# Reordering scores, x transposes, exponentials and masks in the opening of a fused attention and feed-forward kernel

## The chip, the cores and the metric

The kernel runs on one core of a Trainium2 chip. The metric is the device time of one execution in microseconds; of several runs the median is given.

## The reference

Sliding-window attention over 8 batches, 8 heads, 576 positions and a head width of 64 (each position sees those at most 32 away), followed by a two-layer feed-forward block with the quick GELU:

```python
scores = scale * np.matmul(q, k.transpose(0, 1, 3, 2))
mask = np.abs(pos[:, None] - pos[None, :]) <= window
scores = np.where(mask, scores, -1000000000.0)
scores = scores - np.max(scores, axis=-1, keepdims=True)
attn = np.exp(scores)
attn = attn / (np.sum(attn, axis=-1, keepdims=True) + 1e-09)
x = (attn @ v).transpose(0, 2, 1, 3).reshape(4608, 512)
h = x @ w_in
out = (h * (1.0 / (1.0 + np.exp(-1.702 * h)))) @ w_out
```

w_in is 512x2048, w_out 2048x512.

## The kernel before, in words

The 4608 rows are cut into 36 units of 128 rows. Four units make a tile of 512 rows, and the feed-forward block works on tiles. One unit goes through these steps:

- `scores(u, tag)`: 24 small matmuls into two PSUM banks (heads of even and of odd number), then two exponentials on ScalarE (L263), one for each bank, into the SBUF tile p.
- `band(u)`: one multiplication by the 0/1 mask on VectorE (L271), over both halves of p. It needs both exponentials.
- `odd_v(u, eng)`: two copies (L216 and L217) that put together the tile vo from the second half of value tile ve of unit u and the first half of that of unit u+1. In the opening most of them are on VectorE, later they are on GpSimd.
- `values(u, tag)`: 16 small matmuls (pv) into two banks, with a column of ones that yields the sums of the softmax.
- `norm(u)`: reciprocal and multiplication on VectorE (L300, L301), which give x. In the two-bank form "t" that is one pair of instructions, in the forms "AC" and "BE" two pairs.
- `x_T2(u, tag, eng)`: eight transposes on TensorE for units u and u+1 (L329) into one bank, and one copy (L67) to xT.

PSUM has eight banks, and the kernel names them: "t" is two banks, then A, C, B, E, LA and LB. A bank that is asked for again can be written once all instructions that read its last content are done.

The layers use a scheme of seven products of half-sized blocks. In layer 1 (`l1_group`) the sums of the x blocks come from `x_sums` on VectorE, and the order on TensorE is products 1, 7, 6, 2, 5, 4, 3; between 7 and 6 ScalarE copies bank A to B and C to an SBUF tile (L67). Layer 2 (`layer2`) is a list of single matmuls, 8 for each product (o<-w,g; o<-b,g; o<-b,gs and so on), that is drawn from with `do(more, n)` to fill TensorE while other engines work. After the 8 matmuls of product 7 come two copies of seeds, by the engine in `seed2` (L67, o<-o and s7o<-o); product 6 accumulates onto the first one. After product 2 a copy (L521) by the engine in `l2eng` takes a quarter of the result to SBUF.

The order is written out by hand. Each engine runs its instructions strictly in the order of the program (`manual_schedule`), and semaphores are set from the data. So the order of the calls in `opening` (units 0 to 7), `first_layer1` and `run` (units 8 to 15 up to `back(2)`) is the order on every engine.

Loads are issued on the GpSimd queue (`load_v`, `load_w2`, `load_kq`), and each one names one of eight semaphores in turn, so that a load also waits for the one eight places ahead of it. Transposes of q and k by DMA and the stores are on SyncE's queue.

Of the kernel before, what the change touches and what calls it, by code (L numbers as in the profile page):

```python
# [19 lines left out]
AF = mybir.ActivationFunctionType  # L20
# [6 lines left out]
class _Kernel:  # L27
# [214 lines left out]

    def scores(self, u, tag):
        kT, q = self.kT[u], self.qT[u]
        nxt = self.k_first if u == self.NU - 1 else self.kT[u + 1][:, :, 0:64]
        if tag == "t":
            sc = self.bank(tag, name="sc")
            sc = [sc[:, 0], sc[:, 1]]  # L250
        else:
            sc = [self.bank(x, name="sc") for x in tag]
        for hp in range(4):
            c = 128 * hp
            for eo in range(2):
                r = slice(64 * eo, 64 * eo + 64)
                lo, hi = sc[eo][0:64], sc[eo][64:128]
                self.mm(lo[:, c:c + 64], kT[r, hp, 0:64], q[r, hp, 0:64], start=(hp == 0))
                self.mm(hi[:, c:c + 128], kT[r, hp, 64:128], q[r, hp, :], start=(hp == 0))
                self.mm(lo[:, c + 64:c + 128], nxt[r, hp, :], q[r, hp, 64:128], start=False)  # L260
        p = self.p[u] = self.sb("p", [128, 2, 8, SQ], BF16, 4)
        for eo in range(2):
            self.nc.scalar.activation(p[:, eo].rearrange("k h s -> k (h s)"), sc[eo], AF.Exp, scale=self.scale)  # L263

    def band(self, u, eng=None):
        p = self.p[u]
# [302 lines left out]
    def opening(self):  # L569

        nc, dve, act, pool = self.nc, self.nc.vector, self.nc.scalar, self.nc.gpsimd
        self.setup()
        dve.memset(self.idle, 0.0)
        dve.memset(self.spark, 0.0)
        for t in self.ve:
            dve.memset(t[:, :, self.D:], 1.0)
        self.load_first("k", 0)
        self.load_first("q", 0)
        make_identity(nc, self.ident)
        act.activation(self.spark, self.spark, AF.Exp)  # L580
        for u in (0, 1, 2):
            self.load_v(u)
        self.load_w1(0)
        self.setup_mask()
        self.load_first("k", 1)
        self.load_first("q", 1)
        self.cut_mask()
        self.load_w1(1)
        self.load_v(3)
        self.load_v(4)  # L590
        self.load_w1(2)
        self.load_four("k")
        self.load_four("q")
        self.load_w1(3)
        self.odd_v(3, pool)
        dve.tensor_copy(self.identh, self.ident)
        self.keep_busy(60, "E", 96)
        self.T_first("k", 0, "AC", (dve, act))
        self.keep_busy(6, "E")
        self.T_first("q", 0, ("LA", "LB"), (dve, act))  # L600
        self.keep_busy(4, "E")
        for u in (5, 6):
            self.load_v(u)
        self.load_w2(0)
        self.load_v(7)
        self.load_v_part(1024, 64)
        self.load_w2(1)
        self.load_v_part(1088, 64)
        for c in (2, 3):
            self.load_w2(c)  # L610
        self.load_kq("k", 8)
        self.scores(0, "t")
        self.scores(1, "AC")
        self.odd_v(0, dve)
        self.odd_v(1, dve)
        self.keep_busy(10, "E")
        self.band(0)
        self.band(1)
        self.values(0, "t")
        self.values(1, "AC")  # L620
        self.norm(0)
        self.norm(1)
        self.keep_busy(6, "E")
        self.x_T(0, "LA", act)
        self.keep_busy(4, "E")
        self.x_T(1, "LB", act)
        self.T_first("k", 1, "AC", (dve, dve))
        h, n, gelus = [], [0], []

        def l1(half, *ds):  # L630
            for d in ds:
                self.layer1_plain(0, d, half, h[n[0] % len(h)])
                n[0] += 1

        self.layer1_plain(0, 0, 0, "B", gelus)
        self.T_first("q", 1, ("LA", "LB"), (dve, act))
        self.layer1_plain(0, 1, 0, "E", gelus)
        h[:] = ["B", "E", "LB", "LA", "B", "E", "LB", "LA"]
        self.scores(2, "t")
        self.scores(3, "AC")  # L640
        self.layer1_plain(0, 2, 0, "LA", gelus)
        self.layer1_plain(0, 3, 0, "LB", gelus)
        self.do(gelus)
        self.band(2)
        self.odd_v(2, dve)
        self.band(3)
        self.keep_busy(4, "t")
        self.values(2, "t")
        self.norm(2)
        self.keep_busy(4, "A")  # L650
        self.values(3, "AC")
        self.norm(3)
        l1(0, 4)
        self.x_T2(2, "A", dve)
        l1(0, 5)
        dve.tensor_copy(self.k_first, self.kT[0][:, :, 0:64])
        dve.tensor_copy(self.v_first, self.ve[0][0:64])
        for i in (3, 1, 2):
            self.w1_sums((i,), 0)
        for u in (8, 9, 10, 11):  # L660
            self.fetch(u)
        l1(1, 0, 1)
        halo = self.kT[4]
        self.T_four("k", "AC", (dve, dve))
        dve.tensor_copy(self.kT[4][:, :, 0:64], halo)
        self.w1_sums((4,), 0)
        l1(1, 2, 3)
        self.T_four("q", "AC", (dve, act))
        l1(1, 4, 5)
        self.odd_v(4, dve)  # L670
        self.scores(4, "t")
        self.scores(5, "AC")
        self.odd_v(5, dve)
        for i in (3, 1):
            self.w1_sums((i,), 1)
        for d, tag in ((6, "B"), (7, "E")):
            self.layer1_plain(0, d, 0, tag, gelus)
        self.do(self.l2, 3)
        self.scores(6, "t")
        self.do(self.l2, 3)  # L680
        self.scores(7, "AC")
        self.do(gelus)
        self.do(self.l2, 2)
        self.band(4)
        self.odd_v(6, dve)
        self.odd_v(7, dve)
        self.band(5)
        self.values(4, "t")
        self.norm(4)
        self.band(6)  # L690
        self.values(5, "AC")
        self.norm(5)
        self.band(7)
        self.do(self.l2, 4)
        self.values(6, "t")
        self.norm(6)
        self.do(self.l2, 4)
        self.values(7, "AC")
        self.norm(7)
        h[:] = "BE"  # L700
        n[0] = 0
        l1(1, 6, 7)
        self.x_T2(4, "A", act)
        self.do(self.l2, 4)
        self.x_T2(6, "t", dve)
        self.do(self.l2, 4)
# [10 lines left out]
    @staticmethod  # L717
    def do(fs, n=99):
        for _ in range(min(n, len(fs))):
            fs.pop(0)()  # L720
# [77 lines left out]
    def run(self):  # L798
        pool, act = self.nc.gpsimd, self.nc.scalar
        self.l2 = self.layer2_plain(0, 0) + self.layer2_plain(0, 1)  # L800
        self.opening()
        self.do(self.x_sums(1))
        late = self.first_layer1()
        more = self.layer2([(i, j) for i in range(1, self.NT) for j in range(2)][:-1], (self.NT - 1, 1))
        do = self.do
        self.l2eng = dve = self.nc.vector
        self.seed2 = act
        self.scores(8, "t")
        self.scores(9, "AC")
        self.turn(14)  # L810
        self.turn(15)
        do(late, 2)
        do(self.l2)
        self.l2 = more
        self.scores(10, "BE")
        do(more, 12)
        self.band(8)
        self.band(9)
        do(late)
        do(more, 4)  # L820
        self.values(8, "t")
        self.values(9, "AC")
        self.odd_v(12, pool)
        self.odd_v(13, pool)
        self.fetch(16)
        self.fetch(17)
        self.norm(8)
        self.norm(9)
        do(more, 8)
        self.band(10)  # L830
        self.scores(11, "BE")
        do(more, 8)
        self.x_T2(8, "t", act)
        self.values(10, "AC")
        self.norm(10)
        do(more, 8)
        self.scores(12, "t")
        self.scores(13, "BE")
        self.band(11)
        self.values(11, "AC")  # L840
        self.norm(11)
        do(more, 4)
        self.scores(14, "t")
        self.x_T2(10, "C", dve)
        self.scores(15, "BE")
        do(self.x_sums(2))
        self.seed2 = dve
        late = self.back(2)
        for t in range(3, self.NT):
            self.front(t, late)  # L850
            late = self.back(t)
        self.l2eng = act
        self.do(late, 2)
        self.do(self.l2, 16)
        self.do(late)
        self.do(self.l2, 999)
# [68 lines left out]
```

## Time and profile before

| | |
|---|---|
| median of 3 runs | 285.92 us (285.83 to 287.61) |
| the profiled execution | 286.05 us, of which the span is 284.3 us |
| TensorE busy | 275.4 us (97%), 3818 matmuls |
| VectorE busy | 217.0 us (76%) |
| ScalarE busy | 193.7 us (68%) |
| GpSimd busy | 128.8 us (45%) |

The profiled execution is 0.13 us above the median, and 1.75 us of its time lie outside the span. In the rows that follow, a line of the timeline gives the start, the time from the first start to the last end, the engine, the line of the kernel, the operation, output and inputs, shapes and the count, and in brackets how long the engine sat idle before it and what ended that. Matmuls overlap: a row's length is longer than the distance to the next row's start, and it is the distance of starts that tells how fast TensorE gets on. Short idle times are not printed, so a late start without a bracket is read from that distance too.

### The profile page before, as it was taken

The page shows a single profiled execution, that of the slowest core. Times are in us where ns is not written, and L with a number is a line of the kernel's source. Part 1 is how long each engine was busy: PE and PEld are TensorE (multiplying, and loading weights), DVE is VectorE, ACT ScalarE, POOL GpSimd, SP SyncE. Part 2 cuts the span into 40 slices and gives each one's busy share as a digit, 9 for nine tenths or more (in the row PEclk, how much of TensorE's full clock was granted, in tenths as well). Part 3 has the DMA queues.
Part 4 walks back from the last instruction along what each step waited for, and adds up shares of the span by engine and source line. Part 5 has one row for each costly group of instructions (what it writes and reads, how often), then busy time and mean ns, then how long its engine had stood idle before and what let it go on. Part 6 is the DMA issues. An engine that isn't in the chain of part 4 may idle for free.

```text
span 284.3 us, 9219 instructions
## 1 busy us (share of the span) xinstructions
PE 275.4 (97%) x3818; PEld 229.8 (81%) x3818; DVE 217.0 (76%) x500; ACT 193.7 (68%) x340; POOL 128.8 (45%) x195
## 2 busy tenths in 40 slices
PE   7799999999999999999999999999999999999994
PEld 7678847776777888888888888888888888888883
DVE  1758896897887978797879887888788878945631
ACT  2467785789787769667966896588758775567410
POOL 8966467897699719749075909330110000000000
PEclk9999999999999999999999999999999999999999
DMA  7999999999999999999999999994422031201033
GB/s 93 186 193 198 186 202 158 195 124 133 133 171 154 182 130 189 150 201 147 194 106 169 141 201 106 194 112 114 130 59 94 3 111 21 76 0 74 2 112 115
DMA packets 147003, 37.38 MB, mean 131 GB/s; under 512 B 133904, under 2 KB 142608, under 8 KB 146960
## 3 DMA queue, kind: packets, MB, share of 16 engines
q0 software_dynamic: 104480, 18.42, 95.0%
q1 hardware_dynamic: 42032, 17.84, 32.6%
q8 instruction: 30, 0.49, 0.7%
q10 hardware_dynamic: 448, 0.52, 0.6%
q14 instruction: 13, 0.11, 0.1%
HBM read 36.83 MB, written 9.44 MB: 163 GB/s over the span
## 4 chain that ended last, share of the span: by engine, by line
PE 87%; DVE 4%; ACT 3%; DMA 2%; issue 1%; POOL 1%; DVEq 0%; ACTq 0%; POOLq 0%
PE h L70 39%; PE o L70 37%; PE pv L70 4%; PE sc L70 3%; DMA ve<-in_v_dram 2%; DVE p L271 2%; DVE x L301 1%; ACT p L263 1%; PE tp L329 1%; ACT L263 1%; PE junk L70 1%; PE tp L189 1%; PE tp L239 1%; POOL ve L199 1%; ACT g L426 1%
## 5 line engine op out<-in xcount | busy, mean ns | idle before, releaser
L426 ACT ACTIVATE g<-h 128x512 f16<-128x512 f32 x128 | 72.2, 598 | 35.8 <-PE h L70 35.0
L70 PEld LDWEIGHTS <-g 128*128 128x128 f16 x576 | 54.3, 98 | 9.9 <-DMA w<-in_moe_w_out_dram 0.4
L70 PEld LDWEIGHTS <-a 128*128 128x128 f16 x512 | 49.3, 97 | 10.9 <-issue 0.8
L70 PE MATMUL h<-xs,a 128*128 128x256 f16 x384 | 57.6, 272 | 0.1
L70 PE MATMUL o<-w,g 128*128 128x256 f16 (+1 forms) x320 | 55.3, 294 | 0.1
L70 PEld LDWEIGHTS <-w 128*128 128x128 f16 x512 | 48.9, 98 | 6.8 <-DVE xT L67 0.2
L70 PE MATMUL h<-xT,w 128*128 128x256 f16 x384 | 54.0, 273 | 0.0
L199 POOL DMA_DIRECT2D ve<-in_v_dram x39 | 33.3, 857 | 37.8 <-issue 30.8
L70 PEld LDWEIGHTS <-gs 128*128 128x128 f16 x384 | 36.8, 98 | 5.3 <-issue 0.4
L263 ACT ACTIVATE p<-sc 128x512 bf16<-128x512 f32 x72 | 36.7, 617 | 3.2 <-PE sc L70 3.1
L70 PE MATMUL o<-b,gs 128*128 128x256 f16 x256 | 37.7, 273 | 0.5 <-ACT o L67 0.5
L70 PE MATMUL o<-b,g 128*128 128x256 f16 x256 | 37.3, 273 | 0.0
L439 DVE TENSOR_TENSOR h<-h,s 128x512 f32<-128x512 f32 x32 | 22.3, 698 | 18.5 <-PE h L70 18.5
L67 ACT COPY h<-h 128x512 f32<-128x512 f32 x32 | 18.8, 588 | 15.9 <-PE h L70 15.5
L131 POOL DMA_DIRECT2D qst<-in_q_dram x35 | 28.1, 805 | 2.3 <-DMA w<-in_moe_w_out_dram 1.7
L131 POOL DMA_DIRECT2D kst<-in_k_dram x31 | 26.5, 856 | 5.7 <-DMA ve<-in_v_dram 3.9
L301 DVE TENSOR_TENSOR x<-pv,rec 128x256 f16<-128x256 f32 (+1 forms) x53 | 27.6, 520 | 1.8
L271 DVE TENSOR_TENSOR p<-p,mask 128x1024 bf16<-128x1024 bf16 x36 | 24.6, 687 | 4.1 <-ACT p L263 4.1
L445 DVE TENSOR_TENSOR h<-h,s 128x512 f32<-128x512 f32 x32 | 22.4, 700 | 4.7 <-PE h L70 4.2
L216 POOL COPY vo<-ve 64x264 int32<-64x264 int32 x29 | 14.0, 482 | 25.8 <-PE pv L70 24.7
L67 ACT COPY s<-h 128x512 f32<-128x512 f32 x32 | 19.2, 599 | 1.3
L70 PE MATMUL h<-xs,w 128*128 128x256 f16 x128 | 19.2, 273 | 0.0
(86 smaller groups left out, 367.6 us busy)
## 6 DMA issues: line engine op xcount, KB each, us to landing
out_dram<-o_sb SPq DMA_DIRECT2D x33, 256.0 KB, 4.0
ve<-in_v_dram POOLq DMA_DIRECT2D x31, 128.0 KB, 6.5
kst<-in_k_dram POOLq DMA_DIRECT2D x25, 128.0 KB, 6.5
qst<-in_q_dram POOLq DMA_DIRECT2D x21, 128.0 KB, 5.9
w<-in_moe_w_in_dram POOLq DMA_DIRECT2D x4, 512.0 KB, 8.2
w<-in_moe_w_out_dram POOLq DMA_DIRECT2D x4, 512.0 KB, 12.3
qst<-in_q_dram POOLq DMA_DIRECT2D x7, 96.0 KB, 6.7
ve<-in_v_dram POOLq DMA_DIRECT2D x10, 64.0 KB, 7.9
```

Source lines behind the costliest of these rows:

```text
L67: (eng.copy if eng is self.nc.scalar else eng.tensor_copy)(out, in_)
L70: self.nc.tensor.matmul(out, lhsT, rhs, start=start, stop=stop, skip_group_check=True)
L131: self.nc.gpsimd.dma_start(t[off:off + n], src[b, :, s:s + n, :].rearrange("h s d -> s h d"))
L189: self.nc.tensor.transpose(tp[64 * (h % 2):64 * (h % 2) + 64, h // 2, j, :], src[:, 4 * i + h, j, :], self.ident)
L199: self.nc.gpsimd.dma_start(t[off:off + n, :, :self.D], self.v[b, :, s:s + n, :].rearrange("h s d -> s h d"))
L216: eng.tensor_copy(words(vo[64:128]), words(self.ve[u % 9][64:128]))
L263: self.nc.scalar.activation(p[:, eo].rearrange("k h s -> k (h s)"), sc[eo], AF.Exp, scale=self.scale)
L271: (eng or self.nc.vector).tensor_mul(pv, pv, msk.to_broadcast([128, 8, 2, SQ]))
L301: dve.tensor_mul(x[:, 4 * at:4 * (at + n), :].rearrange("p (b h) d -> p b h d", b=n), acc[:, :, :, :D], r.to_broadcast([128, n, 4, D]))
L426: act.activation(g[:, f, 256 * half:256 * half + 256], bank.rearrange("p (i n) -> p i n", i=2), AF.Gelu_apprx_sigmoid)
L439: dve.tensor_add(e, b, s7)
L445: dve.tensor_add(c, b, s7)
```

## The change

Seven edits, all in the order of work of units 4 to 15:

1. In the loads of the opening, `load_w2(0)` goes ahead of `load_v(6)`.
2. `odd_v(5)` goes behind two sums of w1 on VectorE.
3. `band(5)` goes directly behind `band(4)`; of the two `odd_v` calls that stood ahead of it, 6 follows it, and 7 goes behind `norm(4)`.
4. The exponentials of unit 10 are taken out of `scores` (parameter `later`) and issued after the seeds that end the next 16 matmuls of layer 2.
5. `x_T2(8)` uses bank A in place of "t", stands 4 matmuls of layer 2 earlier, and `scores(12)` stands directly behind it.
6. `values(10)` uses B and E in place of A and C; `band(11)` goes ahead of `norm(10)`; `scores(13)` goes behind `norm(11)`, and so directly behind `values(11)` on TensorE.
7. `l2eng` is ScalarE in this stretch, which moves one copy (product 2 of layer 2) from VectorE.

```diff
-    def scores(self, u, tag):
+    def scores(self, u, tag, later=None):
...
+        def exp(eo):
+            self.nc.scalar.activation(p[:, eo].rearrange("k h s -> k (h s)"), sc[eo], AF.Exp, scale=self.scale)
+
         for eo in range(2):
-            self.nc.scalar.activation(p[:, eo].rearrange("k h s -> k (h s)"), sc[eo], AF.Exp, scale=self.scale)
+            exp(eo) if later is None else later.append(lambda eo=eo: exp(eo))
...
-        for u in (5, 6):
-            self.load_v(u)
+        self.load_v(5)
         self.load_w2(0)
+        self.load_v(6)
         self.load_v(7)
...
-        self.odd_v(5, dve)
         for i in (3, 1):
             self.w1_sums((i,), 1)
+        self.odd_v(5, dve)
...
         self.band(4)
+        self.band(5)
         self.odd_v(6, dve)
-        self.odd_v(7, dve)
-        self.band(5)
         self.values(4, "t")
         self.norm(4)
+        self.odd_v(7, dve)
         self.band(6)
...
-        self.scores(10, "BE")
+        exps = []
+        self.scores(10, "BE", later=exps)
         do(more, 12)
...
         do(more, 4)
+        do(exps)
         self.values(8, "t")
...
         self.scores(11, "BE")
-        do(more, 8)
-        self.x_T2(8, "t", act)
-        self.values(10, "AC")
+        self.l2eng = act
+        do(more, 4)
+        self.x_T2(8, "A", act)
+        self.scores(12, "t")
+        do(more, 4)
+        self.values(10, "BE")
+        self.band(11)
         self.norm(10)
         do(more, 8)
-        self.scores(12, "t")
-        self.scores(13, "BE")
-        self.band(11)
         self.values(11, "AC")
         self.norm(11)
+        self.scores(13, "BE")
         do(more, 4)
+        self.l2eng = dve
         self.scores(14, "t")
```

## The prediction

> **What bounds the kernel now.** I read the page first, and then the timelines of three engines in the two stretches that the change touches.
>
> ```profile
> span 284.3 us, 9219 instructions
> ...
> PE 275.4 (97%) x3818; PEld 229.8 (81%) x3818; DVE 217.0 (76%) x500; ACT 193.7 (68%) x340; POOL 128.8 (45%) x195
> ```
>
> TensorE is busy 97% of the span, so only time in which it stands still, or is slowed by a change of the matmul's shape, can be won. Two stretches have such time: 35 to 43 us (masks and values of units 4 to 7) and 72 to 84 us (units 8 to 15 ahead of the first layer-1 group). Behind 84 us nothing is edited, so whatever shift is left at that point reaches the end.
>
> The first stretch, on VectorE, and what TensorE and ScalarE do beside it:
>
> ```profile
> 35.97 0.69 DVE L271 TENSOR_TENSOR p<-p,mask 128x1024 bf16<-128x1024 bf16 x1 [1.43 <-ACT p L263]
> 36.69 0.46 DVE L216 COPY vo<-ve 64x264 int32<-64x264 int32 x1
> 37.18 0.29 DVE L217 COPY vo<-ve 64x264 int32<-64x264 int32 x1
> 37.50 0.55 DVE L216 COPY vo<-ve 64x264 int32<-64x264 int32 x1
> 38.07 0.29 DVE L217 COPY vo<-ve 64x264 int32<-64x264 int32 x1
> 38.29 0.68 DVE L271 TENSOR_TENSOR p<-p,mask 128x1024 bf16<-128x1024 bf16 x1
> 38.89 0.19 DVE L300 RECIPROCAL rec<-pv 128x8 f32<-128x8 f32 x1
> ...
> 39.72 0.68 DVE L271 TENSOR_TENSOR p<-p,mask 128x1024 bf16<-128x1024 bf16 x1
> ...
> 41.42 0.68 DVE L271 TENSOR_TENSOR p<-p,mask 128x1024 bf16<-128x1024 bf16 x1
> ```
>
> ```profile
> 39.02 0.22 PE L70 MATMUL pv<-ve,p 128*64 128x65 bf16 x1 [0.35 <-DVE p L271]
> ...
> 42.15 0.22 PE L70 MATMUL pv<-ve,p 128*64 128x65 bf16 x1 [0.28 <-DVE p L271]
> ```
>
> ```profile
> 34.78 4.09 ACT L263 ACTIVATE p<-sc 128x512 bf16<-128x512 f32 x8
> ```
>
> The reader is to see two things. TensorE waits for masks before the values of unit 5 (39.02) and of unit 7 (42.15). And VectorE runs from 35.97 to the mask of unit 7 at 41.42 without a pause: each row starts where its forerunner leaves off. The values of unit 7 come at the end of that string, so the end of the string sets the stretch, not the wait at 39.02.
>
> The second stretch:
>
> ```profile
> 72.27 1.04 PE L70 MATMUL o<-b,g 128*128 128x256 f16 x8
> ...
> 73.75 0.19 PE L70 MATMUL pv<-vo,p 128*64 128x65 bf16 x1
> 74.40 1.03 PE L70 MATMUL o<-b,gs 128*128 128x256 f16 x8 [0.46 <-ACT o L67]
> 75.36 0.45 PE L70 MATMUL sc<-qT,kT 64*64 64x64 bf16 x24
> 75.74 1.05 PE L70 MATMUL o<-w,g 128*128 128x256 f16 x8
> 76.62 0.61 PE L329 MATMUL tp<-identh,x 128*128 128x128 f16 x8
> ...
> 79.75 0.61 PE L70 MATMUL o<-b,gs 128*128 128x256 f16 x4
> ...
> 80.97 0.62 PE L329 MATMUL tp<-identh,x 128*128 128x128 f16 x8 [0.24 <-DVE x L301]
> ...
> 81.90 0.61 PE L70 MATMUL h<-xT,w 128*128 128x256 f16 x4
> ...
> 82.84 0.61 PE L70 MATMUL h<-xs,a 128*128 128x256 f16 x4
> ...
> 83.64 0.61 PE L70 MATMUL h<-xs,a 128*128 128x256 f16 x4
> ```
>
> ```profile
> 72.93 1.14 ACT L263 ACTIVATE p<-sc 128x512 bf16<-128x512 f32 x2
> 73.90 0.45 ACT L67 COPY o<-o 128x256 f32<-128x256 f32 x1
> 74.20 0.44 ACT L67 COPY s7o<-o 128x256 f32<-128x256 f32 x1
> ...
> 79.04 4.04 ACT L263 ACTIVATE p<-sc 128x512 bf16<-128x512 f32 x8 [0.76 <-PE sc L70]
> 82.97 0.60 ACT L67 COPY h<-h 128x512 f32<-128x512 f32 x1
> ```
>
> ```profile
> 75.64 0.42 DVE L301 TENSOR_TENSOR x<-pv,rec 128x256 f16<-128x256 f32 x1
> ...
> 76.31 0.68 DVE L271 TENSOR_TENSOR p<-p,mask 128x1024 bf16<-128x1024 bf16 x1
> 76.91 0.42 DVE L67 COPY o_sb<-o 128x256 f32<-128x256 f32 x1
> 77.53 0.18 DVE L300 RECIPROCAL rec<-pv 128x4 f32<-128x4 f32 x1 [0.20 <-PE pv L70]
> ...
> 78.63 0.68 DVE L271 TENSOR_TENSOR p<-p,mask 128x1024 bf16<-128x1024 bf16 x1
> 79.73 0.18 DVE L300 RECIPROCAL rec<-pv 128x4 f32<-128x4 f32 x1 [0.42 <-PE pv L70]
> ...
> 81.63 0.69 DVE L67 COPY xT<-tp 128x1024 f16<-128x1024 f16 x1 [0.71 <-PE tp L329]
> ```
>
> Here product 6 of layer 2 (74.40) stands 0.46 us behind a seed copy that ScalarE starts at 73.90, because the exponentials of unit 10 lie ahead of it (72.93, x2). Further on, the x transposes of units 10 and 11 (80.97) wait 0.24 us for the norm of unit 11, and the layer-1 products 7 (82.84) and 6 (83.64) follow the copies at 81.63 (VectorE) and 82.97 (ScalarE), each of which starts as late as the chain ahead of it.
>
> **The opening (edits 1 to 3).** In before, one load of w2 is late:
>
> ```profile
> 35.43 0.33 PEld L70 LDWEIGHTS <-g 128*128 128x128 f16 x3 [0.40 <-DMA w<-in_moe_w_out_dram]
> ```
>
> ```profile
> ve<-in_v_dram POOLq DMA_DIRECT2D x2, 128.0 KB, 11.0
> ```
>
> ```profile
> 20.79 1.89 POOL L199 DMA_DIRECT2D ve<-in_v_dram  x2
> ```
>
> *Load order.* The second of the two value loads (unit 6) is issued about 21.8 and lands 11.0 later, near 32.8; the w2 block behind it ends TensorE's wait at 35.43. It is four times as big, so the 2.6 us between them make some 0.65 us for 128 KB (estimate). Behind the change the block lands near 34.7, the wait of 0.40 us goes, and unit 6 lands near 35.4. Who waits for that is the second copy of `odd_v(5)`, which takes the first half of unit 6. It now stands right ahead of mask 4; with 0.29 (the copy at 37.18) it ends at about 35.7, and mask 4 starts at 35.97, so it is just covered, by 0.27 us. TensorE's 0.40 is not won either: `scores(6)` waits for the second exponential of unit 4 and `values(4)` for those of unit 6, so it only moves slack. GpSimd's later loads exchange semaphores: the first load of k, eight places on, then waits for the w2 block (near 34.7) and not for unit 6, but it isn't used before layer 1 of tile 1, well behind this stretch. Price of both edits: nothing, at most 0.6 if the cover fails (below).
>
> *Masks.* Eight exponentials take 4.09, the last one of them 0.60, so one starts every 0.50. The second of unit 4 ends at 34.78 + 0.50 + 0.60 = 35.88, and its mask starts at 35.97, 0.09 behind. The second of unit 5 ends at 36.88, so mask 5 can't start before 36.97. In before VectorE took up the copies of `odd_v(6)` at 36.69: 0.28 us of pause come into a string that had none. The copies then start at 36.97 + 0.72 (as 35.97 to 36.69) = 37.69; they and the next take 0.79 (37.50 to 38.29): 38.48, when values 4 are done (they start near 38.0, once the sixth exponential frees "t" at 37.88). The norm takes 0.83 (38.89 to 39.72), `odd_v(7)` follows at 39.31, with 0.79 mask 6 comes at 40.10, against 39.72. So the string is 0.38 us later, and mask 7 and values 7 with it: 42.53. The values of unit 5 could start some 0.4 earlier (their banks are freed by the exponentials of unit 7, 38.38 and 38.88), but TensorE gives that back in front of values 6. Bounds: 0.28 (the pause alone) to 0.52 (0.12 more before each copy pair, as 0.72 against the 0.60 from 38.29 to 38.89), and -0.05, if the first copies of the pairs (0.46 and 0.55) fall to the 0.29 of the second ones, 0.43 less. I take +0.38, nearest to the rows.
>
> **Units 8 to 15 (edits 4 to 7).** *Seeds first.* ScalarE is free for the first seed at 72.93; product 7 ends at 72.27 + 1.04 = 73.31. The copies then start at 73.3 and 73.6 (distance 0.30) and the first is over at 73.76. Product 6 starts when the values of unit 9 are out, at 73.75 + 0.19 = 73.94: 0.46 won. The exponentials of unit 10 start at 73.9 and are over at 75.0; `scores(11)`, which could start at 73.94 + 0.96 = 74.90 (74.40 to 75.36), waits for them until about 75.05. That gives 0.15 back.
>
> *Transposes and scores 12.* Scores 0.38 (75.36 to 75.74), 4 matmuls 0.44 (half of 75.74 to 76.62): the transposes come at 75.87. Unit 9's x is complete at 75.64 + 0.42 = 76.06, and its four transposes would start at 76.09: covered. With 0.55 for the eight (0.61 at 76.62 less the overlap), scores 12 start at 76.42, 4 more matmuls at 76.80, values 10 at 77.34. Mask 10 stays at 76.31, since VectorE is full up to there; mask 11 takes the place of the copy at 76.91, which goes to ScalarE. Values 10 (taken as the 0.38 of a group of scores) and 8 matmuls (0.96) bring values 11 to 78.68. In before they filled the 0.38 ahead of the row at 79.75, from 79.37: 0.69 earlier. The norm of unit 11 follows (79.73 less 0.69 = 79.04; norm 10, 1.10 long from 77.70, is over at 78.80). Scores 13 start at 78.95, 4 matmuls at 79.33, scores 14 at 79.87, the transposes at 80.28, when the norm is done (80.97 less 0.69). So product 7 of layer 1 comes at 82.15 by VectorE.
>
> *ScalarE.* Scores 13 are done at 78.95 + 0.45 = 79.40, for ScalarE about 79.45. From there six exponentials at 0.49 (eight from 79.04 to 82.97) run through, and the copy for product 6 starts at 79.45 + 2.95 = 82.40, against 82.97. That is 0.57 earlier, less than 0.69: ScalarE sets the end of the stretch, where VectorE and ScalarE were level. The moved copy (0.30 here) lies ahead of exponential 13 and is covered by the idle time in front of 79.04. I take -0.55; bounds -0.26 (rival three) and -0.69.
>
> In these sums the move of `scores(12)` costs one more change of shape. Ahead of scores 11 eight matmuls take 0.96 (74.40 to 75.36), and 0.88 ahead of 76.62, where no change of shape follows: 0.08 for the way in. No quoted row shows the way out alone; with as much and a half again I put one more group of scores at 0.2 us (estimate). The Trainium skill, in TensorEngine Tiling (Array Packing), section Tiling Modes, says that changing the tiling mode drains TensorE, which speaks against this edit; the trace agrees, with that 0.08. By that rule alone, with no wait removed, the second stretch would cost 0.2 us rather than bring 0.55.
>
> **Sum.** 0.38 - 0.55 = -0.17. The profiled execution took 286.05: 285.88. It stands 0.13 above the median of 285.92, so on the scale of medians the forecast is 285.75 us.
>
> **The rivals.** *One: VectorE's string gets shorter.* The copies of `odd_v` fall to 0.29, the opening ends 0.05 earlier, and the second stretch brings 0.69: 285.92 - 0.74 = 285.2. For it speaks that the copies' lengths differ (0.29 to 0.55) for the same shape; against it that nothing in the edits removes a cause that the rows name. *Two, on the other side: the value load of unit 6 comes late.* If it lands over 0.27 us behind 35.4, the copy of `odd_v(5)` holds up mask 4, and all of VectorE's string with it. One transfer's time more (0.65 to 0.87, the latter a third of 2.6) costs up to 0.6: opening +0.98, in all +0.43, 286.35. For it speaks the thin cover; against it that the bytes ahead of unit 6 are the same that lay ahead of the w2 block. *Three: the second stretch keeps the seeds' gain alone.* If TensorE is set by its own stream, it wins 0.46 and pays 0.20 for the added group: -0.26, with the opening +0.12, 286.05. For it speaks that every wait removed has another one 0.1 to 0.2 behind it; against it that both 80.97 and 82.84 hang on unit 11's values, which move by 0.69.
>
> **How the numbers follow.** Forecast 0.45 (alone 285.4 to 286.1), rival one 0.20, two 0.15, three 0.15, and 0.05 for something not in this list. The range takes in the bounds: below, rival one and the wait of 0.35 before values 5 on top, 284.8; above, rival two with the longer copies (0.14), 286.5. One per cent is 2.9 us, about what a measurement of this kernel can tell from no change; all four cases lie well inside it. Faster by over 1%: 0.01; slower: 0.04, most of the unlisted; within: 0.95.
>
> **What would show it.** Right: no wait before product 6 near 73.9; transposes of units 10 and 11 near 80.3 without a wait; layer-1 product 6 near 83.1, plus the opening's shift. In the opening: mask 5 at about 36.97 with a pause in front, mask 6 near 40.1 and values 7 near 42.5. Wrong: values 7 at 42.1 or sooner (rival one), mask 4 later than 35.97 behind a wait for a value load (rival two), or a table load on ScalarE between exponentials, of which the second stretch has none in the rows from 72.93 to 74.20.

## The result, and the profile after

| | before | after |
|---|---|---|
| median, 20 runs each on one chip | 286.12 us (285.65 to 287.61) | 287.98 us (286.36 to 289.62) |
| the profiled execution | 286.05 us | 287.52 us |
| its span | 284.3 us | 285.7 us |

The ratio is 1.0058, with a 95% interval from 1.0044 to 1.0072: the change costs 1.66 us (0.0058 x 286.12; 1.26 to 2.06). (A ratio here, and in the tables below, isn't the quotient of the two medians, which would be 1.0065.) The loss lies within 1%, as predicted (and as all the cases of the prediction did), but a small gain was forecast, and 287.98 is outside the range of 284.8 to 286.5. The profiled execution gives 1.47 of it.

The head of the page after:

```profile
span 285.7 us, 9219 instructions
...
PE 275.8 (97%) x3818; PEld 229.9 (80%) x3818; DVE 216.2 (76%) x499; ACT 193.9 (68%) x341; POOL 128.5 (45%) x195
```

The counts will matter: VectorE has one instruction less (499 against 500) and ScalarE one more (341 against 340), the copy of edit 7. No other count differs.

The first stretch after, from the timeline of VectorE, and then TensorE's values of units 6 and 7:

```profile
36.50 0.69 DVE L275 TENSOR_TENSOR p<-p,mask 128x1024 bf16<-128x1024 bf16 x1 [1.04 <-ACT p L264]
37.41 0.69 DVE L275 TENSOR_TENSOR p<-p,mask 128x1024 bf16<-128x1024 bf16 x1 [0.22 <-ACT p L264]
38.13 0.29 DVE L216 COPY vo<-ve 64x264 int32<-64x264 int32 x1
...
38.98 0.21 DVE L304 RECIPROCAL rec<-pv 128x8 f32<-128x8 f32 x1 [0.23 <-PE pv L70]
...
40.72 0.67 DVE L275 TENSOR_TENSOR p<-p,mask 128x1024 bf16<-128x1024 bf16 x1
...
42.40 0.68 DVE L275 TENSOR_TENSOR p<-p,mask 128x1024 bf16<-128x1024 bf16 x1
```

```profile
41.44 0.22 PE L70 MATMUL pv<-ve,p 128*64 128x65 bf16 x1 [0.77 <-DVE p L275]
...
43.14 0.22 PE L70 MATMUL pv<-ve,p 128*64 128x65 bf16 x1 [0.28 <-DVE p L275]
```

The string from mask 4 to mask 7, without a pause in before (35.97 to 41.42, 5.45 us), now has two: 0.22 before mask 5, as predicted, and 0.23 before the norm of unit 4 (38.98), which was not. It takes 5.90 (36.50 to 42.40). That it also starts 0.53 later has another cause, shown further down.

The second stretch after, on TensorE, ScalarE and VectorE:

```profile
73.26 1.04 PE L70 MATMUL o<-b,g 128*128 128x256 f16 x8
...
74.86 1.05 PE L70 MATMUL o<-b,gs 128*128 128x256 f16 x8
...
81.35 0.62 PE L333 MATMUL tp<-identh,x 128*128 128x128 f16 x8
...
83.22 0.61 PE L70 MATMUL h<-xs,a 128*128 128x256 f16 x4
...
84.11 0.60 PE L70 MATMUL h<-xs,a 128*128 128x256 f16 x4
```

```profile
74.38 0.36 ACT L67 COPY o<-o 128x256 f32<-128x256 f32 x1 [0.32 <-PE o L70]
...
79.39 0.39 ACT L67 COPY o_sb<-o 128x256 f32<-128x256 f32 x1
80.53 3.04 ACT L264 ACTIVATE p<-sc 128x512 bf16<-128x512 f32 x6 [0.75 <-PE sc L70]
83.42 0.64 ACT L67 COPY h<-h 128x512 f32<-128x512 f32 x1
```

```profile
77.29 1.28 DVE L275 TENSOR_TENSOR p<-p,mask 128x1024 bf16<-128x1024 bf16 x2
```

From product 7 of layer 2 to product 6 of layer 1 before took 11.37 us (72.27 to 83.64), after takes 10.85 (73.26 to 84.11): 0.52 won. Product 6 of layer 2 (74.86) has no bracket any more, the moved copy (79.39) fits in front of an idle time of 0.75, and masks 10 and 11 follow each other (x2).

Behind 84 us, where nothing is edited, two things are late. The first is one addition on VectorE; before and then after, each with the products on TensorE:

```profile
212.55 0.70 DVE L439 TENSOR_TENSOR h<-h,s 128x512 f32<-128x512 f32 x1 [0.74 <-PE h L70]
```

```profile
212.72 0.71 PE L70 MATMUL o<-b,gs 128*128 128x256 f16 x5
213.30 0.60 PE L70 MATMUL h<-xs,a 128*128 128x256 f16 x4
```

```profile
213.31 0.70 DVE L443 TENSOR_TENSOR h<-h,s 128x512 f32<-128x512 f32 x1 [1.09 <-PE h L70]
```

```profile
213.13 0.71 PE L70 MATMUL o<-b,gs 128*128 128x256 f16 x5
214.07 0.60 PE L70 MATMUL h<-xs,a 128*128 128x256 f16 x4 [0.23 <-DVE h L443]
```

VectorE sits idle 1.09 instead of 0.74 us, 0.35 more, and TensorE's shift grows from 0.41 (212.72 to 213.13) to 0.77 (213.30 to 214.07). The second is the end. Issues of the last stores (KB each, microseconds from issue to landing), before and after:

```profile
out_dram<-o_sb SPq DMA_DIRECT2D x1, 128.0 KB, 2.0
out_dram<-o_sb ACTq DMA_DIRECT2D x1, 128.0 KB, 1.7
```

```profile
out_dram<-o_sb SPq DMA_DIRECT2D x1, 128.0 KB, 2.9
out_dram<-o_sb ACTq DMA_DIRECT2D x1, 128.0 KB, 2.4
```

The same stores take 0.9 and 0.7 us longer. In one table, from the rows shown:

| stretch in the profiled execution | shift gained there | rows |
|---|---|---|
| up to mask 4 | +0.53 | 35.97, 36.50 |
| mask 4 to values 7 | +0.46 | 42.15, 43.14 |
| values 7 to layer-1 product 6 | -0.52 | 83.64, 84.11 |
| from there to 213 us | -0.06 | 212.72, 213.13 |
| the addition at 213 us | +0.36 | 213.30, 214.07 |
| from there to the end | +0.63 | spans 284.3, 285.7 |
| sum | +1.40 | |

### The profile page after: what moved, and what is told of

Its sections match the earlier page's. It is cut to its first block, busy times and chain, and to the rows that moved or that the text cites. A ratio compares the mean times of both kernels' runs of the same rounds, so it can differ in the third digit from the quotient of the medians.

```text
span 285.7 us, 9219 instructions
## 1 busy us (share of the span) xinstructions
PE 275.8 (97%) x3818; PEld 229.9 (80%) x3818; DVE 216.2 (76%) x499; ACT 193.9 (68%) x341; POOL 128.5 (45%) x195
## 4 chain that ended last, share of the span: by engine, by line
PE 91%; ACT 3%; DVE 2%; DMA 2%; issue 1%; POOLq 0%
PE h L70 40%; PE o L70 39%; PE sc L70 4%; PE pv L70 4%; DMA kq<-in_k_dram 2%; ACT p L264 1%; PE tp L168 1%; PE tp L333 1%; PE junk L70 1%; PE tp L189 1%; PE tp L239 1%; DVE p L275 1%; DVE x L305 1%; ACT g L401 1%; DVE h L443 0%
```

## The experiments

The theory: the opening costs about 0.45 (masks), the second stretch gains about 0.5, and what turns that gain into a loss lies behind 84 us. The rivals: the load order costs it (prediction's rival two); the gain of the second stretch isn't real; the rest is chance of the loads.

**Which half.** Edits 1 to 3 alone:

```diff
-        for u in (5, 6):
-            self.load_v(u)
+        self.load_v(5)
         self.load_w2(0)
+        self.load_v(6)
...
-        self.odd_v(5, dve)
         for i in (3, 1):
             self.w1_sums((i,), 1)
+        self.odd_v(5, dve)
...
+        self.band(5)
         self.odd_v(6, dve)
-        self.odd_v(7, dve)
-        self.band(5)
...
+        self.odd_v(7, dve)
```

> Edits 1 to 3 alone. The whole change was 1.66 us slower over many runs. If the opening's masks (+0.4 us on VectorE's string) and the load order are where it comes from and the second stretch gains 0.5, this kernel is 2 us slower than before. If the second stretch is the loss, it is 0.4 slower at most. In the profile mask 5 has a pause of about 0.3 in front and values 7 come 0.4 later, measured from mask 4.

Edits 4 to 7 alone (the rest of the change's diff, the opening as before):

> Edits 4 to 7 alone. If the opening is the loss: 0.5 us faster than before, product 6 of layer 2 without a wait, and the layer-1 product 6 ahead of group 0 of tile 2 some 0.5 earlier than before, measured from the start of the scores of units 8 and 9. If the second stretch is the loss: 1 us or more slower.

The whole change without edit 1:

```diff
-        self.load_v(5)
+        for u in (5, 6):
+            self.load_v(u)
         self.load_w2(0)
-        self.load_v(6)
```

> The change with edit 1 undone (value load of unit 6 ahead of the w2 block again). If the late value load is the cause: back to about 285.9, at most 0.3 above before. If the masks or the second stretch are the cause, still 1.2 us or more slower.

The whole change without edit 3:

```diff
-        self.band(5)
         self.odd_v(6, dve)
+        self.odd_v(7, dve)
+        self.band(5)
...
-        self.odd_v(7, dve)
```

> The change with edit 3 undone (the two odd_v between masks 4 and 5 again). If the masks' order is the cause: 0.4 us better than the change, so 1.2 slower than before, or all of it if its effect is larger than the one profile shows. If the load order is the cause: as slow as the change.

| against before on the same chip (286.59) | median | ratio, 95% |
|---|---|---|
| edits 1 to 3 | 286.81 | 1.0005 (0.9986 to 1.0024) |
| edits 4 to 7 | 286.97 | 1.0022 (0.9997 to 1.0047) |
| all but edit 1 | 287.31 | 1.0030 (1.0009 to 1.0051) |
| all but edit 3 | 286.78 | 1.0017 (0.9996 to 1.0038) |

Without edit 1 the kernel is still slower, so the load order doesn't carry the loss. Nothing is faster, the second stretch alone included, though its profile shows the 0.52 again (its rows stand at 73.14 and 83.99, a distance of 10.85). In that profile the two late places behind 84 us are there as well; in that of edits 1 to 3 neither is. So they come with the second half, which ends 130 us ahead of the first of them.

**Which edit of that half.** What differs that far behind is the number of instructions on VectorE and ScalarE. Before with edit 7's copy alone:

```diff
         self.scores(11, "BE")
+        self.l2eng = act
         do(more, 8)
+        self.l2eng = dve
         self.x_T2(8, "t", act)
```

> The kernel before with one copy of layer 2 (product 2 of the first pair, edit 7) on ScalarE in place of VectorE and nothing else. If the count of instructions ahead decides when a block of program code is loaded: a late start of 0.35 us on VectorE near 213 us and a tail behind the last matmul that is 0.5 longer, 0.5 to 1 us slower in all. If the tail and the late start belong to chance: no difference.

Before with one instruction more on ScalarE and VectorE untouched, an exponential of one element for each partition in the opening:

```diff
         act.activation(self.spark, self.spark, AF.Exp)
+        act.activation(self.spark, self.spark, AF.Exp)
```

> The kernel before with the first tiny exponential on ScalarE issued twice, which adds one instruction to ScalarE and none elsewhere. If the count on ScalarE moves the code load at the end: the tail 0.5 longer, no late start of VectorE near 213 us. If the copy itself matters: tail and time as before.

The whole change without edit 7, and edits 4 to 6 alone:

```diff
-        self.l2eng = act
...
-        self.l2eng = dve
```

> The change with edit 7 undone, so that VectorE and ScalarE have as many instructions as before. If the code loads are the cause: tail as before, no late start near 213 us, 0.9 us better than the change, within 0.4 of before. If they are chance: as slow as the change.

> Edits 4 to 6 alone, on the opening of before. If masks and code loads are the two costs: 0.4 to 0.6 us faster than before. If the second stretch has a cost of its own: as before or slower.

| against before on the same chip (286.59) | median | ratio, 95% | late add at 213 us | last SyncE store of 128 KB |
|---|---|---|---|---|
| the copy alone | 287.38 | 1.0030 (1.0016 to 1.0045) | yes | 2.7 |
| one more on ScalarE | 287.42 | 1.0035 (1.0014 to 1.0057) | no | 2.7 |
| all but edit 7 | 287.29 | 1.0015 (0.9993 to 1.0037) | no | 1.9 |
| edits 4 to 6 | 286.95 | 1.0016 (1.0001 to 1.0030) | no | 1.9 |

The copy alone, which moves no wait of TensorE in the stretch where it stands (11.37 us there, as in before), costs 0.86 us (0.0030 x 286.59; 0.46 to 1.29). Its two rows, VectorE's addition and the store:

```profile
213.26 0.70 DVE L439 TENSOR_TENSOR h<-h,s 128x512 f32<-128x512 f32 x1 [1.09 <-PE h L70]
```

```profile
out_dram<-o_sb SPq DMA_DIRECT2D x1, 128.0 KB, 2.7
out_dram<-o_sb ACTq DMA_DIRECT2D x1, 128.0 KB, 2.4
```

One exponential of 0.2 us at 2 us into the kernel makes the last stores late and not the addition: the tail hangs on ScalarE's count, the addition on VectorE's.

Edits 4 to 6 show what edit 7 is for. VectorE, then TensorE:

```profile
77.91 0.42 DVE L67 COPY o_sb<-o 128x256 f32<-128x256 f32 x1 [0.46 <-PE o L70]
78.25 0.68 DVE L275 TENSOR_TENSOR p<-p,mask 128x1024 bf16<-128x1024 bf16 x1
```

```profile
80.09 0.44 PE L70 MATMUL sc<-qT,kT 64*64 64x64 bf16 x21 [0.30 <-DVE x L305]
...
84.12 0.60 PE L70 MATMUL h<-xs,a 128*128 128x256 f16 x4
```

Left on VectorE, the copy waits 0.46 for its product, mask 11 and both norms stand behind it, and `scores(13)` waits 0.30 for x. Product 7 starts at 72.73 there, so the distance to 84.12 is 11.39: against 11.37 the whole gain is gone. The copy that costs the tail is the one without which the stretch gains nothing.

**The counts kept.** If the counts are the cause, the copy can stay on ScalarE as long as both counts are as before at the two late places: one `memset` more on VectorE in the opening, and the two exponentials of unit 12 as one instruction of 128x1024 on ScalarE (the same values).

```diff
         dve.memset(self.spark, 0.0)
+        dve.memset(self.spark, 0.0)
...
+        if u == 12:
+            self.nc.scalar.activation(p.rearrange("k e h s -> k e (h s)"), both, AF.Exp, scale=self.scale)
+            return
```

With edits 4 to 7, and with the whole change:

> Edits 4 to 7 on the opening of before, with the counts of before on both engines: one more tiny memset on VectorE in the opening, and the two exponentials of unit 12 as one instruction over both banks, one fewer on ScalarE. If the counts place the code loads: the second stretch keeps its 0.5 us, tail and VectorE near 213 us as before, 0.5 us faster than before. If the copy itself makes the late start and the tail: 0.4 slower.

> The whole change with the same two compensations. If the counts place the code loads: the change less 0.9 us, so the masks' 0.4 to 0.9 against the second stretch's 0.5: 0 to 0.4 slower than before. If not: 1.6 slower.

The whole change with the `memset` alone, one run:

> The whole change with one more tiny memset on VectorE alone. If each engine's count places its own code loads: no late start of 0.35 us on VectorE near 213 us, but the tail still 0.5 longer, which belongs to ScalarE.

Edit 3 alone:

> Edit 3 alone on before: both odd_v behind mask 5. If VectorE's string sets the opening: values 7 come 0.4 to 0.9 later, measured from the exponentials of unit 4, and the time is 0.4 to 0.9 longer. If the earlier values 5 count: no longer, or shorter by up to 0.35.

| against before on the same chip (286.77) | median | ratio, 95% | late add | last SyncE store |
|---|---|---|---|---|
| edits 4 to 7, counts kept | 286.95 | 0.9993 (0.9967 to 1.0019) | no | 1.9 |
| the change, counts kept | 286.34 | 0.9993 (0.9967 to 1.0019) | no | 1.9 |
| the change and the memset | 286.96 (one run) | | no | 2.6 |
| edit 3 alone | 287.33 | 1.0030 (1.0001 to 1.0058) | no | 1.9 |

With both counts restored the whole change is no longer measurably slower, and in its profile and that of edits 4 to 7 both late places are gone. With VectorE's alone the addition is in time again and the tail stays late:

```profile
213.16 0.70 DVE L443 TENSOR_TENSOR h<-h,s 128x512 f32<-128x512 f32 x1 [0.74 <-PE h L70]
```

```profile
out_dram<-o_sb SPq DMA_DIRECT2D x1, 128.0 KB, 2.6
out_dram<-o_sb ACTq DMA_DIRECT2D x1, 128.0 KB, 2.1
```

The other edits' prices can be read from all the profiles. In the nine profiles with the old order of masks, the string from mask 4 to mask 7 takes 5.04 to 5.47, mean 5.31; in the eight with edit 3, 5.50 to 6.09, mean 5.84. Edit 3 costs 0.54 us (0.60 without the four kernels with the `memset`, which has a price of its own, shown next). The stretch from product 7 to product 6 is 10.85 to 10.86 in all nine profiles with edits 4 to 7, and 11.39 in both without the copy.

**What one would keep.** Edits 1, 2 and 4 to 7 with both counts kept (no mask move), the change again, and before again, on one chip:

> Edits 1, 2 and 4 to 7 (all but the masks) with the counts of before on both engines. If the second stretch's 0.5 us reaches the end: 0.4 to 0.6 faster than before. If the late k transposes at 107 and 135 us, seen in some profiles, take it back: no faster than before, with waits for kT in the profile.

> The change once more on this chip. If the sum of masks (0.4 to 0.9), second stretch (-0.5) and code loads (0.35 and 0.5 to 0.6) is the cause: 0.7 to 1.5 us slower than before, the late start of VectorE near 213 us and the long tail in this profile too.

> The kernel before once more. The time of before, within 0.4 us; if the waits for the third piece of w_in and for late k transposes belong to the machine and not to the edits, at least the first of them appears in this profile too.

| against before on the same chip (286.56) | median | ratio, 95% |
|---|---|---|
| without edit 3, counts kept | 286.89 | 1.0008 (0.9987 to 1.0029) |
| the change again | 288.15 | 1.0054 (1.0030 to 1.0078) |
| before again | 286.78 | 0.9999 (0.9976 to 1.0023) |

The change's loss repeats (1.55 us; 0.86 to 2.24). The version that keeps the gain and has neither late place isn't faster than before, though its profile has the distance of 10.86. Its interval reaches down to 0.9987, a gain of 0.37 us, so the whole 0.52 of the stretch did not reach the end of these runs. One reason stands in its profile, at mask 4:

```profile
35.11 4.03 ACT L264 ACTIVATE p<-sc 128x512 bf16<-128x512 f32 x8
```

```profile
36.71 0.69 DVE L278 TENSOR_TENSOR p<-p,mask 128x1024 bf16<-128x1024 bf16 x1 [1.03 <-ACT p L264]
```

Mask 4 starts 1.60 us behind the first of these exponentials. In before it is 1.19 (34.78 and 35.97), and so it is in all thirteen profiles without the `memset`; in all four with it, it is 1.60. From the `memset` to the moved copy VectorE's count is one higher than in before, and 0.41 us are lost at mask 4. TensorE's shift against before grows from 0.34 at 30 us to 0.70 behind values 7 here; in edits 4 to 7 with counts kept it stays at 1.24, with copies on VectorE that are all short. So the counts were restored at the late places, but a new one came up in between; a filler right beside the moved copy was not run. No version here beats before.

## Why the prediction was wrong

**The failed step** is "Behind 84 us nothing is edited, so whatever shift is left at that point reaches the end", and with it the price of edit 7, "covered by the idle time". The copy is covered where it stands (79.39, ahead of 0.75 idle). But one instruction fewer on VectorE and one more on ScalarE cost 0.35 and about 0.55 us where nothing was edited. (The tail, from the last matmul's start to the end of the span, is 0.47 to 0.64 longer than in before in the six profiles with both counts changed, and 0.60 and 0.31 in the two with ScalarE's count alone.) That makes the sign of the result: with +0.54 and -0.52, edits 3 and 4 to 7 would have come out even, and with the counts kept they do (0.9993).

That the counts decide is shown: in all six profiles with 499 instructions on VectorE the addition at 213 us waits the 0.35 longer, in none of the eleven with 500; in all eight with 341 on ScalarE the last SyncE store takes 2.5 to 2.9 us, in none of the nine with 340 more than 2.0. How it comes about is less sure. The loads of program code are queues of their own in the profile; the page after has them as

```profile
q8 instruction: 30, 0.49, 0.7%
...
q14 instruction: 13, 0.11, 0.1%
```

and they move with the counts. Queues of the window 208 to 208.6 us of before, and of 214.3 to 215 of after:

```profile
q14 instruction: 1, 0.01, 3.2%
```

```profile
q14 instruction: 1, 0.01, 2.9%
```

In each window the other kernel has no such row, and neither the `memset` nor the exponential kernel has one at 214.3. So a block of code of some 8 KB (0.11 MB by 13) is loaded 6 us later, and VectorE is late just ahead of it. It holds in all profiles: the load starts between 208 and 211 us in the eleven with 500 instructions on VectorE and between 214 and 217 in the six with 499. The late mask 4 fits in by its place: counted in the trace with VectorE's waiting instructions, it is the 64th instruction in the four kernels with the `memset`, and the late addition is the 448th in the six, 384 (three times 128) further. The place alone isn't enough, though, for the 64th in after is mask 5, which isn't late. At the end, the load of a block stands against the last stores. ScalarE's store of 128 KB, issued in before, in after, and in the kernel with one exponential more at

```profile
280.93 0.36 ACTq L467 DMA_DIRECT2D out_dram<-o_sb  x1
```

```profile
281.69 0.36 ACTq L471 DMA_DIRECT2D out_dram<-o_sb  x1
```

```profile
281.40 0.36 ACTq L467 DMA_DIRECT2D out_dram<-o_sb  x1
```

Queues of 282.4 to 282.9 us of before, 282.5 to 283.0 of after, and 281.8 to 282.4 of the third:

```profile
q14 instruction: 1, 0.01, 4.5%
```

```profile
q14 instruction: 1, 0.01, 3.9%
```

```profile
q14 instruction: 1, 0.01, 6.9%
```

In before the store lands near 282.6 (280.93 and 1.7), so that it has at most 0.2 us to go when the load starts. By the same 1.7 the store of after would land at 283.4, and has 0.4 to 0.9 to go; that of the third at 283.1, and has 0.7 or more. Counted from the last matmul's start, this load comes 2.1 to 2.4 us later in the nine profiles with 340 instructions on ScalarE, and 1.2 to 1.6 in the eight with 341. That the load holds up the store is argued from this order; no run moved the load alone. Nor does a run show why a block's load at 208 costs VectorE nothing and one at 214 costs 0.35.

The Trainium skill, in Runtime: NRT & Kernel Launch, section Instruction fetch mechanics, says that an engine fetches its code ahead in blocks through a DMA queue of its own, and that crossing a block's boundary is mostly hidden. The traces agree that it mostly is (13 loads on q14 in after, and two places of loss), but here the two that weren't decided the sign. Of a queue for each engine they show less: the load that moves with VectorE's count and the one that moves with ScalarE's are both on q14.

**The masks (0.38 predicted).** Right in the main mechanism, a pause that makes the string longer, and near in after itself: 5.90 us, where 5.45 and 0.38 make 5.83. The pause before mask 5 came as said (0.22 for 0.28). The mean price is larger, 0.54, because the string of the old order takes 5.31 on average and not the 5.45 of before: copies can be short there. The step "they and the next take 0.79 (37.50 to 38.29): 38.48, when values 4 are done" carries the long copies of before over. In after the copies took 0.29 (the row at 38.13), VectorE was done early and waited 0.23 for those values. So faster copies didn't help, as rival one had it; they turned into that wait. In the old order they do help: 5.04 to 5.47 by their lengths.

Against rival one the prediction says that nothing in the edits removes a cause that the rows name. Rows of GpSimd that it doesn't show name one; in before they are

```profile
35.67 1.35 POOL L131 DMA_DIRECT2D qst<-in_q_dram  x2 [1.74 <-DMA w<-in_moe_w_out_dram]
37.01 0.94 POOL L131 DMA_DIRECT2D kst<-in_k_dram  x1
```

The long copies (36.69, 0.46 long, and 37.50, 0.55 long) each start while GpSimd issues a load, and end about 0.1 us behind the end of that row. Between 32 and 46 us of all profiles, a copy beside which GpSimd issues nothing takes 0.29 or 0.30 us, and every longer one has such an issue beside it, though not every issue makes a copy longer (37.18, 0.29). In after the copies of `odd_v(6)` come behind these issues. That the issue holds up the copy is argued from this order; no run moved a load alone.

**The load order (0 predicted).** Right within what can be told. The copy of `odd_v(5)` did wait for unit 6's values, 0.46 in after:

```profile
35.13 0.33 DVE L217 COPY vo<-ve 64x264 int32<-64x264 int32 x1 [0.46 <-DMA ve<-in_v_dram]
```

It was still done at 35.46, and mask 4 came 1.04 later behind its exponentials (36.50). The cover held, even where the copy waited longest for the load (1.06, in the change without edit 7: mask 4 still waited 0.44 behind it for its exponentials), and rival two falls. The wait of 0.40 for the w2 block, which edit 1 was to take away and the sum took as no gain, stands only in the profiles of before and of the copy alone; before again doesn't have it. The change without edit 1 (1.0030; 1.0009 to 1.0051) can't be told from the change.

**The second stretch (-0.55 predicted).** Right: -0.52, in every profile to 0.01, and by the mechanism told: product 6 without a wait, masks 10 and 11 in one, ScalarE's copy for product 6 following six exponentials. Counted from product 7 of layer 2, the transposes come 0.61 earlier (80.97 - 72.27 and 81.35 - 73.26; 0.69 predicted) and ScalarE's copy 0.54 (82.97 - 72.27 and 83.42 - 73.26; 0.57 predicted), and it is ScalarE that sets the end. (The sum gives four matmuls ahead of values 10 0.54 without a row for it; in after they take as much, from 77.78 to 78.32.) Rival three (the seeds' gain alone) falls.

**What stays open.** The terms +0.54, -0.52, +0.35 and +0.55 make +0.92; measured are 1.66 (1.26 to 2.06) and 1.55 (0.86 to 2.24). The change without edit 1, which has all four terms, measured 0.86 (0.26 to 1.46). With the `memset` at 0.41, the intervals of the other kernels hold the sums of their terms as well, but for edits 4 to 6, where the terms make 0 and the interval starts at 1.0001. The fastest of the 20 runs of before and after differ by 0.71 (286.36 and 285.65), near the sum, and the medians by 1.86: what is missing lies in the slower part of the runs. Loads may have a part in it. The weights of w_in at 23 to 24 us, in after, before again, and edits 4 to 7 alone, where the opening is that of before:

```profile
23.38 0.77 PEld L70 LDWEIGHTS <-w 128*128 128x128 f16 x8 [0.92 <-DMA w<-in_moe_w_in_dram]
```

```profile
23.00 0.77 PEld L70 LDWEIGHTS <-w 128*128 128x128 f16 x8 [0.26 <-DMA w<-in_moe_w_in_dram]
```

```profile
23.97 0.77 PEld L70 LDWEIGHTS <-w 128*128 128x128 f16 x8 [1.40 <-DMA w<-in_moe_w_in_dram]
```

These waits come up with the opening of before too and differ from one execution to the next; the +0.53 ahead of mask 4 comes from them. A second place is the scores at 136 us, which in edits 4 to 7 alone waited 0.73 for a transposed k (kT<-kst). From layer-1 product 6 to 212 us TensorE took 0.56 longer in before again than in before, 2.07 longer in edits 4 to 7 alone and 2.14 in the change with counts kept, though nothing is edited there. Whether the change makes such waits more frequent isn't settled: one execution of each kernel is in a profile.

## What to carry to other kernels

Moving an instruction from one engine to another has a price apart from its place: it changes both engines' counts, and with them the points at which their code is loaded, up to the end of the program. Where tenths of a microsecond matter, compare the rows far behind the last edit too (an addition's idle time, the landing of the last stores), and try the edit with both counts kept before judging it. Keep them at every place where an engine is waited for, and not only in sum: a filler at the start of the program shifts everything up to the edit. A pause put into a full string isn't paid by the instructions that get faster behind it, if the next of them waits for another engine.

## What the runs showed of the hardware that was not expected

- A code block's loading point moves 6 us for one instruction (208 to 214 us), and an engine can start 0.35 us late next to it.
- One exponential of 0.2 us at the start of the program made the last 128 KB store land after 2.7 us, not 2.0, some 280 us later, and the time 0.35% longer (0.14 to 0.57).
- One `memset` more on VectorE in the opening made a mask some 35 us further on start 0.41 us late, in four of four profiles.
- Copies of one shape (64x264) on VectorE took 0.29 to 0.73 us, the same copy 0.29 and 0.67 in two executions of before; those beside which GpSimd issued no load took 0.29 or 0.30. The string of masks took 5.04 to 5.47 in the old order with them.
